# The range test of w1 and the squares of pairs 0 to 7 move from the first two stages to later fetches in the last ones

## The chip, the cores and the metric

The kernel runs on one core of a Trainium2 chip. The core has five engines, each with its own instruction stream: TensorE (PE in the profile; its weight loads are PEld), VectorE (DVE), ScalarE (ACT), GpSimd (POOL) and SyncE (SP). Data come from and go to device memory by DMA; here SP and POOL issue the transfers. The metric is the device time of one execution in microseconds (us), the median of several runs.

## The reference

A hashed attention over 4 batches, 8 heads, 768 rows and a head size of 64 gives x; a Fourier mixing block with two weight matrices works on x. Cut to what matters:

```python
mask = q_bucket[:, :, :, None] == k_bucket[:, :, None, :]     # 6 sign bits of q @ proj, k @ proj
scores = np.where(mask, scale * np.matmul(q, k.transpose(0, 1, 3, 2)), -1e9)
attn = softmax(scores)                                        # with the maximum subtracted
x = (attn @ v)  ->  (B, S, H*D)

u = x + np.real(np.fft.fft(np.fft.fft(x, axis=1), axis=2))
un = (u - mean) / np.sqrt(var + 1e-6)
out = u + np.maximum(un @ w_ch1, 0.0) @ w_ch2                 # w_ch1 512x2048, w_ch2 2048x512
```

Both weight matrices arrive as 64-bit floats. The kernel reads them as pairs of 32-bit words and makes 32-bit floats of them.

## The kernel before

The work is cut by batch. `attention(b)` handles the 4 head pairs of a batch (pair number n = 4b + t), each in 6 steps of 128 keys: `weigh` makes the scores (line 893; for the first pairs the mask is a product too, line 885), ACT takes their exp into one of two `pk` tiles (L897), and `values` multiplies by v (L914). The exp is taken without subtracting a maximum, which holds only for inputs of moderate size. `mix(b)` then does the Fourier part (`fold`, the products L1086 into F, L1115 into x) and `mlp7`, the two weight products in a scheme with seven products for eight. `mix(b)` of one batch is interleaved with `attention(b + 1)` by a counter in the main loop (L1500 to L1548). The last `mix(3)` has no attention beside it and runs alone: this is the last stage, from about 925 us on.

Two safety tests guard the fast path. If either fires, a slower general version of the whole computation (`_any_scores`) runs afterwards.

- The range test. `narrow` (L628) turns a raw slice of 128 x 512 double words into floats: two DVE instructions (L639, L643), one on ACT (L647), one on DVE (L649), and then, on ACT, the test: `Abs` of the high word (L654) and `Relu` of a threshold minus it (L655), summed into a column of `strange`. There are 16 slices of w1 (`weights1`, in the first stage, fetched by SP into seven raw buffers) and 16 of w2 (`weights2`, in the second stage, fetched by POOL, L693, into two).
- The norm test. `norm` (L748) squares a natural q or k tile of 128 x 768 on ACT (L750) and sums it into a column of `norms`; `prepare(n)` calls it for q and for k of each pair.

After the last attention, just before `mix(3)`, both tables are reduced (L1523 to L1538: two DVE reductions, three PE transposes, five small DVE instructions) to one flag, and `values_load` (L1539) puts it into a register of each engine.

Order. In the first stage (`attention(0)` with `weights1`, up to about 135 us) the order of PE, DVE, ACT and POOL is that of the program. From then on a scheduler in the compiler orders each engine's list at build time from its own estimates; the engines then run their lists in that order. SP's list is ordered by it throughout.

Buffers that matter. The tag `qkn` has two buffers for q and k tiles. The tag `z` has one: raw slices of w1, then z of each batch in turn (read by L1086), with raw slices of w2 in between. PSUM banks for products come from `pt` (L520): two banks normally; with `roomy` set (first stage's start, and from L1519 on) its requests rotate over three pools of two.

In `mlp7`, `inner(half)` has 4 row blocks in each half, of 7 products each (A11, S2, A12, S1, S3, S4, A22; L1390). ACT copies each result out of PSUM (L1412 c12, L1415 c21, L1419 c11, L1422 c22, L1427 and L1439 sd, L1431 c12), and A12, S4 and A22 add onto banks that must have been copied before. The left operands come from device memory by SP through a ring of 12 tiles (L1363). `outer7` has 8 products for each of 3 row pairs and half (L1270), with ACT copies L1289, L1300 and L1303 into `tq`. `across` transposes x into row tiles `un`, and ACT copies them out (L1142).

Of the kernel before, what the change touches and what calls it, by code (L numbers as in the profile page):

```python
# [20 lines left out]
P = 128  # L21
# [464 lines left out]
def _main(  # L486
# [27 lines left out]
    def wt(shape, dtype, tag, name, bufs=2):  # L514
        return work.tile(shape, dtype, tag=tag, name=name, bufs=bufs)
# [105 lines left out]


    least = const.tile([P, 1], F32, tag="least", name="least")
    nc.gpsimd.memset(least, float(897 << 20))
    strange = const.tile([P, 2 * NDC * DFF // WC], F32, tag="strange", name="strange")
    nc.gpsimd.memset(strange, 0.0)

    def narrow(dst, raw, col, low=None):  # L628


        lo, hi = (raw[..., i] for i in range(2))
        t = lo.bitcast(F32)
        if low is None:

            low, t = lo, hi.bitcast(F32)
        di = dst.bitcast(I32)


        nc.vector.tensor_scalar(  # L639
            di, hi, 3, (1 << 30) - 1,  # L640
            op0=ALU.logical_shift_left, op1=ALU.bitwise_and,
        )
        nc.vector.scalar_tensor_tensor(  # L643
            di, hi, -(1 << 30), di, op0=ALU.bitwise_and, op1=ALU.bitwise_or
        )

        nc.scalar.activation(low, lo.bitcast(U32), AF.Copy, scale=2.0**-29)  # L647
        if len(di.shape) == 2:
            nc.vector.tensor_tensor(di, di, low, op=ALU.add)  # L649
        else:  # L650
            for i in range(di.shape[1]):
                nc.vector.tensor_tensor(di[:, i], di[:, i], low[:, i], op=ALU.add)

        nc.scalar.activation(t, hi, AF.Abs)  # L654
        nc.scalar.activation(  # L655
            t, t, AF.Relu, bias=least, scale=-1.0, accum_out=strange[:, col : col + 1]
        )
# [22 lines left out]
    class Arrival:  # L680
# [19 lines left out]
        def convert(self, i, low=None):  # L700
            if self.wide:
                dst = self.slices[i][0]
                raw = self.raws[i % self.depth].bitcast(I32)
                if len(dst.shape) == 2:
                    raw = raw.rearrange("p (n w) -> p n w", w=2)
                else:
                    raw = raw.rearrange("p (s n w) -> p s n w", w=2, n=dst.shape[-1])
                narrow(dst, raw, self.col + i, low)
            self.fetch(i + self.depth)

    def weights1():
        slices = [
            (w1[:, c, f : f + WC], moe_w_ch1[c * P : (c + 1) * P, f : f + WC])
            for f in range(0, DFF, WC)
            for c in range(NDC)
        ]
        zt = wt([P, 3, 2 * WC], F32, "z", "zraw1", 1)
        ft = wt([P, 12, WC], F32, "F", "fraw", 1)
        raws = [zt[:, i] for i in range(3)] + [
            ft[:, i : i + 2].rearrange("p i w -> p (i w)") for i in range(0, 8, 2)  # L720
        ]
        arrival = Arrival(slices, raws, 0, nc.sync)
        for i in range(arrival.depth):
            arrival.fetch(i)
            if i == 1:
                load(1)
        yield
        half = None
        for i in range(len(slices)):
            arrival.convert(i, ft[:, 8 + i % 4].bitcast(I32))  # L730
            yield
            if half:
                centre(half[0], next(half[1]))
                half = None
            if i % NDC == NDC - 1:


                f = i // NDC * WC
                if f < DFF // 2:
                    half = f, average(f)  # L740
                    next(half[1])
# [2 lines left out]
    xs = {}  # L744

    preps = {}

    def norm(n, io, tn):  # L748
        junk = wt([P, S], BF16, "junk", f"sq{io}_{n}", 1)
        nc.scalar.activation(  # L750
            junk, tn, AF.Square,
            accum_out=norms[:, io, n : n + 1],
        )

    def prepare(n):
# [3 lines left out]
        for io, nm in enumerate("qk"):  # L759
            tn = nat.pop((nm, n))  # L760
            tt = wt([P, S], F32, nm + "t", f"{nm}t{n}")
            if n > 0:
                to, at = tt, tn
                if nm == "q":

                    to = tt.rearrange("p (i r n) -> p r i n", i=2, r=2)
                    at = tn.rearrange("p (r i n) -> p r i n", i=2, r=2)
                nc.vector.transpose(to, at)
            for g in range(2) if n == 0 else ():
                ps = pt([P, 3, P], f"tr{nm}{n}_{g}")  # L770
                for i in range(3):
                    c = 2 * i + g if nm == "q" else 3 * g + i
                    nc.tensor.transpose(ps[:, i, :], tn[:, c * P : (c + 1) * P], ident)
                if nm == "q":
                    for i in range(2):
                        dst = tt[:, i * HALF + g * HALF // 2 : i * HALF + (g + 1) * HALF // 2]
                        evac(
                            dst.rearrange("p (j c) -> p c j", c=3),
                            ps[:, :, i * D : (i + 1) * D],
                        )  # L780
                else:
                    evac(
                        tt[:, g * HALF : (g + 1) * HALF],
                        ps.rearrange("p c t -> p (c t)"),
                    )
            ts[nm] = tt
            yield
            norm(n, io, tn)
        if lite:


# [708 lines left out]
    for b in range(B):  # L1500
# [17 lines left out]
        if b == B - 1:  # L1518
            roomy[0] = True  # L1519

            ms = const.tile([P, 3], F32, tag="ms", name="ms")  # L1523
            nc.vector.tensor_reduce(ms[:, 0:2], norms, axis=AX.X, op=ALU.max)
            nc.vector.tensor_reduce(ms[:, 2:3], strange, axis=AX.X, op=ALU.max)
            ps = pt([1, 3, P], "norms_t")
            for io in range(3):
                nc.tensor.transpose(ps[:, io, :], ms[:, io : io + 1], ident)
            mt = const.tile([1, 5], F32, tag="mt", name="mt")
            nc.vector.tensor_reduce(mt[:, 0:3], ps, axis=AX.X, op=ALU.max)  # L1530
            nc.vector.tensor_tensor(mt[:, 3:4], mt[:, 0:1], mt[:, 1:2], op=ALU.mult)
            nc.vector.tensor_scalar(
                mt[:, 4:5], mt[:, 3:4], (SAFE / SCALE / 2) ** 2, None, op0=ALU.is_gt
            )
            fl = const.tile([1, 1], I32, tag="fl", name="fl")
            nc.vector.scalar_tensor_tensor(
                fl, mt[:, 2:3], 0.0, mt[:, 4:5], op0=ALU.is_gt, op1=ALU.max
            )  # L1538
            large = nc.values_load(fl[0:1, 0:1], min_val=0, max_val=1)  # L1539
        for _ in other:  # L1540
            pass
        other = mix(b)
        if b == 0:
            zt2 = wt([P, 3, 2 * WC], F32, "z", "zraw2", 1)
            arrival2 = weights2()
            other = after(2 + NT, other, islice(arrival2, HF + 1))
    for _ in other:
        pass  # L1548

    return large  # L1550

# [42 lines left out]
```

## Time and profile before

| | us |
|---|---|
| median of 3 runs (1101.38 to 1104.4) | 1102.72 |
| the profiled execution | 1102.7 |
| its span, first to last instruction | 1100.4 |
| PE busy | 1043.3 |
| DVE busy | 790.5 |
| ACT busy | 499.5 |
| POOL busy | 58.6 |

The groups that the change moves, from the answers on single lines (counts and median duration in ns): L654 Abs 32 x 686, L655 Relu 32 x 772, L750 square 32 x about 843. The counts of L654 and L655 include w2's 16 slices; w1's are those from 15.4 to 94 us. The squares of pairs 0 to 7 are 16 of the 32, from 7.3 to 182 us.

How to read it: a busy share is an average over stages with different limits, so each stage is looked at by itself. In a timeline a line gives start, duration, engine, line of the code and operation; the bracket at its end is the idle time of the engine before it and what ended that. In the table by windows the columns are the window, its length, then busy time of PE, PEld, DVE, ACT and POOL, the granted clock, the mean busy share of the 16 DMA engines and what they moved in GB/s.

### The profile page before, as it was taken

The page shows a single profiled execution, that of the slowest core. Times are in us where ns is not written, and L with a number is a line of the kernel's source. Part 1 is how long each engine was busy: PE and PEld are TensorE (multiplying, and loading weights), DVE is VectorE, ACT ScalarE, POOL GpSimd, SP SyncE. Part 2 cuts the span into 40 slices and gives each one's busy share as a digit, 9 for nine tenths or more (in the row PEclk, how much of TensorE's full clock was granted, in tenths as well). Part 3 has the DMA queues.
Part 4 walks back from the last instruction along what each step waited for, and adds up shares of the span by engine and source line. Part 5 has one row for each costly group of instructions (what it writes and reads, how often), then busy time and mean ns, then how long its engine had stood idle before and what let it go on. Part 6 is the DMA issues. An engine that isn't in the chain of part 4 may idle for free.

```text
span 1100.4 us, 14144 instructions
## 1 busy us (share of the span) xinstructions
PE 1043.3 (95%) x4933; PEld 632.7 (57%) x4933; DVE 790.5 (72%) x1336; ACT 499.5 (45%) x1055; POOL 58.6 (5%) x132
## 2 busy tenths in 40 slices
PE   7989897999989999999999999999999999999996
PEld 3333353446744675545664576645674569768575
DVE  5899958878599977776767785965856785644353
ACT  6987555553276324454326433355315522340420
POOL 0000000002000020010000011001000002100000
PEclk9999999999999999999999999999999999999998
DMA  9755353451056161322154134213032205122301
GB/s 222 224 95 126 64 140 72 138 164 19 20 149 209 44 204 26 68 63 66 26 157 107 48 82 153 44 43 92 15 129 68 68 24 172 55 81 88 123 20 41
DMA packets 175710, 103.13 MB, mean 94 GB/s; under 512 B 129552, under 2 KB 162960, under 8 KB 175632
## 3 DMA queue, kind: packets, MB, share of 16 engines
q1 hardware_dynamic: 169840, 88.65, 30.1%
q0 software_dynamic: 4224, 13.11, 3.7%
q8 instruction: 41, 0.67, 0.2%
q10 hardware_dynamic: 1568, 0.39, 0.2%
q14 instruction: 37, 0.30, 0.1%
HBM read 81.14 MB, written 20.97 MB: 93 GB/s over the span
## 4 chain that ended last, share of the span: by engine, by line
PE 61%; DVE 11%; ACT 4%; DMA 2%; issue 2%; DVEq 0%; SPq 0%; ACTq 0%
PE o L1270 22%; PE h_p L1390 20%; PE oo L914 6%; PE sc L893 6%; DVE pk L903 3%; PE cs L1086 2%; DMA zraw<-in_moe_w_ch_dram 2%; PE A L1115 2%; PE B L1115 1%; DVE acc L988 1%; ACT rr L948 1%; DVE w L1282 1%; DVE h L1256 1%; PE bits L825 1%; PE un L1141 1%
## 5 line engine op out<-in xcount | busy, mean ns | idle before, releaser
L1270 PE MATMUL o<-w,h 128*128 128x256 f32 x1152 | 259.4, 382 | 1.2 <-ACT tq L1289 0.7
L1270 PEld LDWEIGHTS o<-w,h 128*128 128x128 f32 x1152 | 216.3, 190 | 43.6 <-issue 4.6
L897 ACT ACTIVATE pk<-sc 128x768 f32<-128x768 f32 x192 | 147.6, 809 | 78.4 <-PE sc L893 60.9
L1390 PE MATMUL h_p<-x,w 128*128 128x384 f32 x448 | 163.5, 495 | 3.2 <-ACT h L1412 1.5
L893 PE MATMUL sc<-qt,kt 64*128 64x384 f32 x768 | 155.7, 508 | 6.0 <-ACT pk L897 5.7
L914 PE MATMUL oo<-pk,vn 128*64 128x385 f32 (+1 forms) x768 | 155.3, 499 | 6.0 <-DVE pk L903 3.0
L903 DVE SCALAR_TENSOR_TENSOR pk<-qb,kb,pk 128x768 f32<-128x768 bf16 x132 | 129.0, 1012 | 30.2 <-ACT pk L897 30.1
L1390 PEld LDWEIGHTS h_p<-x,w 128*128 128x128 f32 x448 | 82.3, 190 | 71.0 <-ACT pk L897 5.4
L988 DVE TENSOR_TENSOR acc<-acc,pk 128x1536 f32<-128x1536 f32 (+1 forms) x72 | 105.7, 1482 | 7.2 <-ACT pk L897 6.7
L1390 PE MATMUL h_p<-w 128*128 128x384 f32 x288 | 105.5, 489 | 2.3 <-ACT w L1427 2.3
L914 PEld LDWEIGHTS oo<-pk,vn 128*64 128x64 f32 x768 | 49.1, 136 | 100.0 <-issue 69.3
L893 PEld LDWEIGHTS sc<-qt,kt 64*128 64x128 f32 x768 | 66.9, 188 | 51.3 <-issue 24.0
L1390 PEld LDWEIGHTS h_p<-w 128*128 128x128 f32 x288 | 53.7, 190 | 41.7 <-ACT w L1427 3.5
L1300 ACT COPY tq<-o 128x256 f32<-128x256 f32 x24 | 8.9, 372 | 105.1 <-PE o L1270 105.1
L1282 DVE SCALAR_TENSOR_TENSOR w<-o,rs,w 128x256 f32<-128x256 f32 x56 | 26.7, 478 | 41.6 <-PE o L1270 41.6
L1270 PE MATMUL o<-w 128*128 128x256 f32 x176 | 42.3, 383 | 1.3 <-DVE w L1282 1.3
L1416 DVE TENSOR_TENSOR h<-h 128x384 f32<-128x384 f32 x32 | 17.8, 556 | 33.1 <-ACT h L1415 33.1
L1289 ACT COPY tq<-o 128x256 f32<-128x256 f32 x24 | 8.9, 371 | 69.3 <-PE o L1270 69.2
L1270 PEld LDWEIGHTS o<-w 128*128 128x128 f32 x176 | 32.8, 190 | 8.8 <-DVE w L1282 2.9
L1423 DVE TENSOR_TENSOR h<-h 128x384 f32<-128x384 f32 x32 | 17.7, 553 | 27.0 <-ACT h L1422 27.0
L1024 POOL DMA_DIRECT2D out_dram<-w x30 | 16.4, 548 | 388.7 <-issue 293.2
L1086 PE MATMUL cs<-ch,z 128*128 128x128 f32 (+3 forms) x192 | 33.2, 324 | 3.0 <-DVE bt L829 1.9
(170 smaller groups left out, 1312.4 us busy)
## 6 DMA issues: line engine op xcount, KB each, us to landing
w<-ad SPq DMA_DIRECT2D x168, 128.0 KB, 2.0
w<-bd SPq DMA_DIRECT2D x42, 512.0 KB, 4.5
zraw<-in_moe_w_ch_dram POOLq DMA_DIRECT2D x16, 512.0 KB, 4.0
bd<-w SPq DMA_DIRECT2D x14, 512.0 KB, 3.9
vn<-in_v_dram SPq DMA_DIRECT2D x32, 192.0 KB, 3.4
qn<-in_q_dram SPq DMA_DIRECT2D x120, 48.0 KB, 2.4
kn<-in_k_dram SPq DMA_DIRECT2D x60, 96.0 KB, 3.4
zraw<-in_moe_w_ch_dram SPq DMA_DIRECT2D x8, 512.0 KB, 5.7
```

What stands on the lines that cost most here:

```text
L893: last[0] = nc.tensor.matmul(ps[:, h, 0:HALF], kt[rows, ks], qt[rows, qs], start=kb is not None, stop=True,)
L897: nc.scalar.activation(pk[:, g, :, 0:HALF], ps[:, :, 0:HALF], AF.Exp, scale=SCALE)
L903: nc.vector.scalar_tensor_tensor(w, qb[:, h].rearrange("p (g s) -> p g s", g=2), kb[:, h, c : c + 1], w, op0=ALU.is_equal, op1=ALU.mult,)
L914: nc.tensor.matmul(oos[g][h * D : (h + 1) * D, 0:w], nat["v", n][:, (2 * c + h) * D : (2 * c + h + 1) * D], pk[:, g, h, 0:w], start=(c == ...
L988: nc.vector.tensor_tensor(acc[:, g], (first if c == 1 else acc)[:, g], new[:, g], op=ALU.add,)
L1086: nc.tensor.matmul(ps[:, pc + 2 * lo : pc + 2 * hi - 1 : 2], z[:, cp, pc, par, t * P : (t + 1) * P], ch[:, cp, pc, lo:hi], start=(cp == 0) ...
L1115: nc.tensor.matmul(ps[:, cols], F[:, par, k, t, j * P : (j + 1) * P], sq[:, t, k, cols], start=(t == 0), stop=(t == 1),)
L1270: nc.tensor.matmul(ps, a[:, r], right7[i][:, r], start=start and r == 0, stop=r == HF // 2 - 1, skip_group_check=not start,)
L1282: nc.vector.scalar_tensor_tensor(t[:, cols], src, r, t[:, cols], op0=ALU.mult, op1=ALU.add)
L1390: nc.tensor.matmul(ps, left[:, k], right[i][:, k], start=start and k == 0, stop=k == 1, skip_group_check=not start,)
L1416: nc.vector.tensor_tensor(c21, c12, c21, op=ALU.add)
L1423: nc.vector.tensor_tensor(c22, c21, c22, op=ALU.add)
```

## The change

The 16 range tests of w1's slices are no longer made when the slices are converted. `Arrival` is given no column (`None`), and `narrow` then leaves the test out. The test itself becomes a function `in_range`, which reads the high word as a 32-bit float instead of as an integer; the threshold is the same bit pattern read as a float. w2's tests stay where they were, in this form.

`prepare(n)` no longer squares q and k of pairs 0 to 7. Pairs 8 to 15 keep their squares.

A new generator `guard` makes up for both. It fetches q and k of pairs 0 to 7 a second time (16 transfers of 128 x 768 floats, 384 KB each, 3 KB in one piece per partition, issued by POOL into the `qkn` buffers) and squares each; it fetches the 16 raw slices of w1 a second time (512 KB each, by POOL, into three raw buffers in the `z` tag) and tests each; and it does the reductions and the flag. In the program it is stepped inside the loop over `mix(3)`; the register load of the flag follows at step 56 of 64.

```diff
-    nc.gpsimd.memset(least, float(897 << 20))
+    nc.gpsimd.memset(least, float(np.array(897 << 20, np.int32).view(np.float32)))
...
+        if col is not None:
+            in_range(raw, col, t)
...
+    def in_range(raw, col, t=None):
+        lo, hi = (raw[..., i].bitcast(F32) for i in range(2))
+        t = lo if t is None else t
         nc.scalar.activation(t, hi, AF.Abs)
         nc.scalar.activation(
             t, t, AF.Relu, bias=least, scale=-1.0, accum_out=strange[:, col : col + 1]
...
-        arrival = Arrival(slices, raws, 0, nc.sync)
+        arrival = Arrival(slices, raws, None, nc.sync)
...
+    LATER = 2 * NPAIR
+    def guard():
+        for n in range(LATER):
+            b, t = divmod(n, NPAIR)
+            for io, src in enumerate((q, k)):
+                tn = wt([P, S], F32, "qkn", f"nn{io}_{n}", 2)
+                nc.gpsimd.dma_start(
+                    tn,
+                    src[b, 2 * t : 2 * t + 2].rearrange("h (p c) d -> (h p) (c d)", p=P // 2),
+                )
+                norm(n, io, tn)
+                yield
+        if wide:
+            raws = wt([P, 3, 2 * WC], F32, "z", "zlast", 1)
+            for i, (dst, src) in enumerate(slices1()):
+                raw = raws[:, i % 3].bitcast(I32)
+                nc.gpsimd.dma_start(raw.bitcast(I64), src)
+                in_range(raw.rearrange("p (n w) -> p n w", w=2), i)
+                yield
...
+        yield fl
...
-            norm(n, io, tn)
+            if n >= LATER:
+                norm(n, io, tn)
...
-    for _ in other:
-        pass
+    checks = guard()
+    flag = None
+    for i, _ in enumerate(other):
+        if (i < 9 or i % 4 < 3) and flag is None:
+            flag = next(checks)
+        if i == MIX - 8:
+            large = nc.values_load(flag[0:1, 0:1], min_val=0, max_val=1)
```

What stands between the `if wide` part and `yield fl` are the reductions and the flag, unchanged, that stood before `mix(3)`.

More of the change, by code (lines that the diff above doesn't have):

```diff
@@ L652, in narrow @@
                 nc.vector.tensor_tensor(di[:, i], di[:, i], low[:, i], op=ALU.add)
+        if col is not None:
+            in_range(raw, col, t)
+    wide = moe_w_ch1.dtype == I64
+    def in_range(raw, col, t=None):
+        lo, hi = (raw[..., i].bitcast(F32) for i in range(2))
+        t = lo if t is None else t
         nc.scalar.activation(t, hi, AF.Abs)
@@ L707, in convert, with slices1 @@
                     raw = raw.rearrange("p (s n w) -> p s n w", w=2, n=dst.shape[-1])
-                narrow(dst, raw, self.col + i, low)
+                narrow(dst, raw, self.col and self.col + i, low)
             self.fetch(i + self.depth)
-    def weights1():
-        slices = [
+    def slices1():
+        return [
             (w1[:, c, f : f + WC], moe_w_ch1[c * P : (c + 1) * P, f : f + WC])
@@ L716, in weights1 @@
         ]
+    def weights1():
+        slices = slices1()
         zt = wt([P, 3, 2 * WC], F32, "z", "zraw1", 1)
@@ L746, in _main @@
     preps = {}
+    LATER = 2 * NPAIR
[17 more added lines that the diff above has]
+                yield
+        ms = const.tile([P, 3], F32, tag="ms", name="ms")
+        nc.vector.tensor_reduce(ms[:, 0:2], norms, axis=AX.X, op=ALU.max)
+        nc.vector.tensor_reduce(ms[:, 2:3], strange, axis=AX.X, op=ALU.max)
+        ps = pt([1, 3, P], "norms_t")
+        for io in range(3):
+            nc.tensor.transpose(ps[:, io, :], ms[:, io : io + 1], ident)
+        mt = const.tile([1, 5], F32, tag="mt", name="mt")
+        nc.vector.tensor_reduce(mt[:, 0:3], ps, axis=AX.X, op=ALU.max)
+        nc.vector.tensor_tensor(mt[:, 3:4], mt[:, 0:1], mt[:, 1:2], op=ALU.mult)
+        nc.vector.tensor_scalar(
+            mt[:, 4:5], mt[:, 3:4], (SAFE / SCALE / 2) ** 2, None, op0=ALU.is_gt
+        )
+        fl = const.tile([1, 1], I32, tag="fl", name="fl")
+        nc.vector.scalar_tensor_tensor(
+            fl, mt[:, 2:3], 0.0, mt[:, 4:5], op0=ALU.is_gt, op1=ALU.max
+        )
+        yield fl
     def norm(n, io, tn):
@@ L1519, in _main @@
             roomy[0] = True
[L1523 to L1539, printed above, removed]
         for _ in other:
```

## The prediction

> **What bounds the kernel now.** I read the page (busy shares, chain of waits) first, then the busy time by windows cut at stage borders, then the timelines of ScalarE (ACT) and VectorE (DVE) in the places that the change touches.
>
> ```profile
> PE 1043.3 (95%) x4933; PEld 632.7 (57%) x4933; DVE 790.5 (72%) x1336; ACT 499.5 (45%) x1055; POOL 58.6 (5%) x132
> ...
> PE 61%; DVE 11%; ACT 4%; DMA 2%; issue 2%; DVEq 0%; SPq 0%; ACTq 0%
> ```
>
> TensorE (PE) holds the chain. The exceptions, by windows (columns: length, then busy PE, PEld, DVE, ACT, POOL, clock, DMA share, GB/s):
>
> ```profile
> 41.00:68.40 27.40, 24.15 (x164) 9.35 (x162) 26.32 (x44) 23.47 (x48) 0.00 (x0) 1.00 0.63 130
> 68.40:99.00 30.60, 28.30 (x192) 11.11 (x190) 28.83 (x49) 29.94 (x64) 0.11 (x1) 1.00 0.50 98
> ...
> 135.00:190.00 55.00, 44.94 (x246) 26.89 (x246) 38.70 (x66) 30.33 (x64) 3.45 (x6) 0.96 0.41 106
> ...
> 932.00:945.00 13.00, 12.59 (x80) 12.14 (x80) 9.64 (x19) 1.65 (x6) 0.00 (x0) 1.00 0.00 1
> 945.00:957.00 12.00, 12.00 (x46) 7.48 (x45) 7.29 (x16) 7.22 (x16) 1.70 (x4) 1.00 0.27 78
> 957.00:970.00 13.00, 13.00 (x42) 7.64 (x41) 4.91 (x11) 6.42 (x14) 3.69 (x9) 1.00 0.33 102
> ```
>
> From 41 to 99 us ACT is nearly full, but so is DVE (its timeline shows back-to-back instructions, one gap of 0.28 us). From 945 PE is full, and ACT, half busy, empties each PSUM bank as its product ends. Prices and waits, from timelines:
>
> ```profile
> 50.54 0.69 ACT L654 ACTIVATE zraw<-zraw 128x512 f32<-128x512 int32 x1
> 51.27 0.81 ACT L655 ACTIVATE zraw<-zraw,least 128x512 f32<-128x512 f32 x1
> ...
> 52.04 1.50 ACT L897 ACTIVATE pk<-sc 128x768 f32<-128x768 f32 x2
> 53.42 0.85 ACT L750 ACTIVATE sq<-kn 128x768 bf16<-128x768 f32 x1
> ...
> 54.25 1.51 ACT L897 ACTIVATE pk<-sc 128x768 f32<-128x768 f32 x2
> ...
> 175.14 0.53 POOL L693 DMA_DIRECT2D zraw<-in_moe_w_ch_dram  x1 [10.93 <-ACT zraw L655]
> ...
> 179.06 0.70 ACT L647 ACTIVATE zraw<-zraw 128x512 int32<-128x512 uint32 x1 [4.22 <-DMA zraw<-in_moe_w_ch_dram]
> ...
> 944.40 0.59 ACT L1142 COPY w<-un 128x512 f32<-128x512 f32 x1 [11.35 <-PE un L1141]
> ...
> 948.50 0.49 ACT L1419 ACTIVATE h<-h_p 128x384 f32<-128x384 f32 x1 [0.81 <-PE h_p L1390]
> ```
>
> Start to next start: a test (Abs, Relu) holds ACT 1.50 us, a square 0.83. A POOL fetch of 512 KB takes 3.9 us, and ACT stands behind it.
>
> **The skill.** "Perfetto Trace Analysis", Tensor Engine Instruction, says ACT and DVE run strictly first in, first out; the wait at 179.06, with a score tile's exp ready behind it, agrees. "DMA: Bandwidth & Descriptors", Anatomy of one DMA, prices a POOL transfer at 2.0 us plus bytes/436e3: 3.2 us for 512 KB; the trace has a median of 4.0 and decides. "ScalarE: Activation LUTs", What ACT_TABLE_LOAD costs, charges per element, whatever the function; Abs 0.69 and Relu 0.77 on 512 elements fit, so reading the words as float should cost what reading them as integers does.
>
> **Part 1, taken away.** 16 tests x 1.50 and 16 squares x 0.83 = 37.3 us of ACT.
> - First stage, up to 135 us: all tests, 13 squares. DVE has gaps of 1.27, 1.66 and 2.43 us before 41 and 0.28 after; to 117 it is then full. The first waits on a conversion with no test ahead of it, the third on PE's sums, themselves behind DVE. Only the second (accumulation at 17.78, its exp queued behind a test until 16.96) closes, by about 1.1. Gain 1.2; bounds 0 and 3.
> - Second stage: two squares stand in the two-buffer ring of w2's fetches, at 172.48 and 181.14. Without them the fetch of 175.14 starts 0.8 earlier and the exp of 181.97 comes 1.65 earlier. The scheduler also puts a second exp ahead of the next waiting conversion (before: 186.13, with PE idle 2.66). Some returns where DVE builds the next operands. Gain 2.0; bounds -1 (reordering) and 8 (most of PE's 10 us idle in 135-190).
> - Before the last stage the reductions, three transposes and flag leave 900-903: about 1 us of DVE, which delayed ACT's rr copies. They return in the last stage's second inner half, where DVE has room. Gain 0.5; bounds 0 and 1.
>
> **Part 2, squares added.** In the changed program's lists they are not in the last mix: the scheduler puts them into the preceding one, ACT's list after the tq copy of 772.84, POOL's after the rs group that ends at 749.9. Two buffers: a fetch waits for the square two before. No row shows 384 KB through POOL. Taking 4.0 x 0.75 = 3.0 as low end and 4.0 as high, I use 3.4. A round of two squares then lasts 3.4 + 0.83 + 0.1 = 4.3 us. The first pair is there; seven rounds give 775 + 7 x 4.3 = 805, and with other work in the way about 809. Walking ACT's list against PE's (product 1.73 us, score or value group 1.45): the copy of o_0_0_6 comes 0.7 us after its bank is needed, that of o_0_1_4 1.3 after; the rest fit, since the scheduler spread attention steps out. Cost 2.0; bounds 0.5 and 6. POOL waits meanwhile; its next task, a store at 888, is far.
>
> **Part 3, tests added.** zlast takes z's buffer, free after the last cs matmul at 932.2. Three fetches go out at 0.53 us spacing. Two issued together at 151.13 were consumed at 155.85 and 157.44, so I let three land at 936.8, 938.4, 940.0. ACT is idle 933.05-944.40 and its list has six tests there: 936.8-941.5 for three; refetches from 938.4, 940.0, 941.6 take about 4.3 and land at 942.7, 944.3, 945.9, so the sixth ends at 947.4. The un copies start 3.0 late. Ten more tests are threaded between PSUM copies up to the third row block's c22 copy (970.3 before). ACT holds about 14.3 us of own work in 944.4-970.3 (7.2 + 6.4 + the ends); with 10 x 1.5 = 15 that is 29.3 in 25.9: 3.4 us over even without a gap. Walking the list with refetch waits (eighth 0.3, fourteenth 1.0) and waits on DVE sums, the copy ends near 977.8: 7.5 late, and PE's next accumulation needs it. Later ACT has 0.8 us free per product, but PE has none, so nothing is recovered. Cost 7.5; low end 1.4 + 3.4 - 0.3 = 4.5 (3.7 us fetches, perfect packing), high 14 (fetches at 5.6, as that of the second raw at 151.8). Cover elsewhere: POOL's rs results wait behind these fetches, but the outer products that need them start at 982; SP's flag load sits ahead of nine ring loads that are wanted a row block (7 products, 9 us) after the flag's; and 8.4 MB over 38 us make 220 GB/s beside the ring's 100, while the window 205-230 moved 234 at a DMA share of 0.65, so the engines just suffice.
>
> **Sum**, against this execution (span 1100.4, time 1102.7, the runs' median 1102.72): -1.2 - 2.0 - 0.5 + 2.0 + 7.5 = +5.8, so span 1106.2 and time **1108.5**.
>
> **Rivals.**
> - *Cancelled* (0.19): tests packed at 4.5, squares 0.5, gains 4.5: 1103.2. For it: six-bank PSUM rotation in the last stage lets PE run a product ahead. Against: c12's copy gates the product after next.
> - *Fetches slow under load* (0.12): 5.6 us each makes a square round 6.5, seven end at 820, 10 late; tests 11: -3.7 + 21 = 1120. For it: 7.5 us seen for the fetch of 163.68. Against: DMA carries about 1 GB/s at 790-810 and 932-945.
> - *Faster* (0.08): the second stage's w2 ring. If 8 of PE's 10 us idle return, with 2.0 of the first stage and 0.5, against costs at their low ends (5.0): -5.5, 1097.2. It decides once the gains pass 8.3. For it: ACT waited 23.3 us there on fetches. Against: the squares held only 1.65 of that ring, its own tests stay.
> - *The test fires* (0.01): the fallback runs and time doubles. The weights are random at a scale of 0.04; the threshold is 2^-126.
>
> **Numbers.** Forecast case 0.60. A measurement here tells 0.3%, 3.3 us, from none: the bounds are 1099.4 and 1106.0. Faster 0.08 (that rival); within 0.20 (most of cancelled, a little of the forecast's low side); slower 0.72. Range 1102.5 to 1117: the known bounds, leaving out the faster rival, the worst of the slow fetches, and the fallback.
>
> **What would show it.** First stage: DVE as full as before, about 1 us shorter. 770-812: sq instructions 2.2 us apart, PE gaps near 2 us. After the F copies: six tests, un copies 3 us late; the first inner half with ACT above 90% and PE idle of some 7 us. I am wrong if the first inner half keeps its length, or the first 230 us shorten by over 6.

## The result, and where the time went

Before 1102.77 us (median of 5 runs, 1101.38 to 1104.4), after 1115.96 us (median of 5, 1113.99 to 1119.01). The ratio is 1.0125, 95% interval 1.0106 to 1.0143: slower, inside the range given, but by 13.2 us where 5.8 were forecast. The profiled execution took 1115.4 us, its span is 1113.5.

The page of the kernel after, busy times and chain of waits:

```profile
PE 1050.3 (94%) x4933; PEld 632.6 (57%) x4933; DVE 789.8 (71%) x1336; ACT 499.8 (45%) x1055; POOL 76.2 (7%) x164
...
PE 20%; DMA 4%; DVE 2%; issue 2%; ACT 1%; POOL 1%; POOLq 0%; DVEq 0%; ACTq 0%
```

PE has the same 4933 products and 7 us more of busy time; ACT has as much work as before, only elsewhere. The chain is cut short (its shares add up to 30%), so its shares cannot be set against those of before; but the two transfers by which its DMA share goes, `nn` and `zlast`, are those that the change added. To see where they cost, I cut the span at five marks that exist in both programs and do not move against each other: the copy of the first outer product of the third `mix` (the copy at 772.84 before), the first copy of a weight product in its second half (827.33), the first F copy of the last stage (926.12), the first outer copy of the last stage (984.48), and the end. All numbers are start times in the timeline of ACT, subtracted.

| stretch, us | before | before, profiled again | after | squares only | w1 tests only | neither |
|---|---|---|---|---|---|---|
| start to outer copy (first two stages and more) | 772.84 | 770.52 | 771.02 | 769.95 | 772.84 | 770.69 |
| to weight product copy (squares are here) | 54.49 | 54.50 | 61.74 | 61.56 | 54.49 | 54.49 |
| to first F copy (flag was here) | 98.79 | 98.79 | 98.46 | 98.47 | 98.45 | 98.79 |
| to outer copy (tests are here) | 58.36 | 58.36 | 66.57 | 58.15 | 68.51 | 58.36 |
| to the end of the span | 115.92 | 115.73 | 115.71 | 115.77 | 115.71 | 115.77 |

Two things are to be seen. The last four rows repeat to 0.2 us between two executions of the kernel before, so for a stretch without the moved checks a difference is real. With them the stretches scatter more: four kernels with the same list of ACT in the squares' stretch (after, squares only, and two that follow) took 61.56, 61.74, 61.84 and 62.58 us there, and four with the same list in the tests' stretch (after, and three that follow) 66.57, 67.37, 67.63 and 68.69. The first row differs by 2.3 us between those same two executions, so a gain of that size in one profile means nothing. The loss has two places and no more: +7.25 us where the squares stand, +8.21 where the tests stand; 0.33 comes back from the flag and 0.21 in the last row.

The same stretches by windows of the kernel after (columns as before). The first three answer to the windows of the first two stages that were shown, the fourth holds the squares, the last two the tests:

```profile
41.00:68.40 27.40, 24.12 (x150) 8.68 (x148) 24.17 (x40) 13.91 (x26) 0.00 (x0) 0.88 0.65 131
68.40:99.00 30.60, 28.88 (x186) 11.15 (x186) 27.51 (x47) 19.23 (x40) 0.11 (x1) 0.94 0.39 82
135.00:190.00 55.00, 46.59 (x260) 27.22 (x256) 41.92 (x73) 30.20 (x63) 3.40 (x6) 1.00 0.43 113
769.20:831.00 61.80, 57.00 (x268) 38.16 (x267) 39.30 (x57) 27.35 (x62) 8.71 (x16) 0.97 0.48 154
...
937.20:953.60 16.40, 13.89 (x84) 12.57 (x82) 11.36 (x20) 9.75 (x22) 4.25 (x8) 1.00 0.69 226
953.60:983.00 29.40, 26.13 (x81) 14.97 (x82) 10.48 (x24) 25.83 (x61) 9.87 (x20) 0.94 0.72 236
```

From 41 to 99 us ACT lost 20 us of work and the stage did not become shorter: the granted clock is 0.88 and 0.94 where it was 1.00, and DVE, which was the next to be full, is idle 2.2 and 1.3 us more. From 769 to 831 PE is idle 4.8 us with ACT busy less than half of the time. From 953.6 to 983, ACT is busy 88% and PE idle 3.3 us. The granted clock is no cause of the two losses, though it fell in both places: in the kernel after it was 0.97 over the whole stretch of the squares, and two kernels with the same squares and 1.00 took as long (61.84 and 62.58 us); over that of the tests it was 0.97 too, and the kernel with the tests alone, at 1.00, took 68.51.

**The squares.** ACT, POOL and DVE in the timeline of the kernel after (start, duration, engine, line, operation; the bracket is the idle time before it and what ended it):

```profile
771.02 0.37 ACT L1342 COPY tq<-o 128x256 f32<-128x256 f32 x1 [2.02 <-PE o L1323]
773.88 0.84 ACT L802 ACTIVATE sq<-nn 128x768 bf16<-128x768 f32 x1 [2.49 <-DMA nn<-in_q_dram]
...
778.55 0.84 ACT L802 ACTIVATE sq<-nn 128x768 bf16<-128x768 f32 x1 [3.73 <-DMA nn<-in_k_dram]
...
779.39 0.35 ACT L1353 COPY tq<-o 128x256 f32<-128x256 f32 x1
...
784.04 0.84 ACT L802 ACTIVATE sq<-nn 128x768 bf16<-128x768 f32 x1 [2.00 <-DMA nn<-in_k_dram]
```

```profile
746.97 1.09 POOL L1205 TENSOR_TENSOR rs<-rs,mhalf 128x1 f32<-128x1 f32 x2
770.43 0.64 POOL L769 DMA_DIRECT2D nn<-in_q_dram  x1 [22.37 <-issue]
775.12 0.54 POOL L769 DMA_DIRECT2D nn<-in_k_dram  x1 [4.05 <-ACT sq L802]
776.12 0.54 POOL L769 DMA_DIRECT2D nn<-in_q_dram  x1 [0.46 <-DVE kt L820]
```

```profile
768.87 0.97 DVE L820 STREAM_TRANSPOSE qt<-qn 128x768 f32<-128x768 f32 x1
...
774.86 0.96 DVE L820 STREAM_TRANSPOSE kt<-kn 128x768 f32<-128x768 f32 x1
...
782.01 1.95 DVE L956 SCALAR_TENSOR_TENSOR pk<-qb,kb,pk 128x768 f32<-128x768 bf16 x2 [3.57 <-ACT vs L977]
```

```profile
784.51 5.41 PE L1323 MATMUL o<-w,h 128*128 128x256 f32 x16 [1.89 <-DVE rt L992]
```

POOL is done with its rs group at 748 and then stands 22 us: the two buffers hold q and k of the last pair, long squared (at 710.52 and 720.00) but transposed only at 768.87 and 774.86. So the first fetch leaves at 770.43, when q's buffer is free. The second, by its bracket, waits for the square made of the first and leaves at 775.12; only the third (776.12) waits for the transposition of k. The first two squares, which I had counted as ready, hold ACT 6.2 us. Behind them stand a copy (779.39, 8.4 us after the one at 771.02; 6.0 us before), two exps and a scale copy, for which DVE waits 3.57 us; PE then waits 1.89 us for DVE. After that the ring runs on; over all sixteen:

```profile
  ACT sq L802: 18.4, 14
...
DMA to landing us min/median/max: 3.1/3.3/4.8
```

ACT waited 18.4 us on these fetches in 14 waits. Each single fetch takes what I had assumed (3.4 us).

**The tests.** ACT in the timeline of the kernel after, from the end of the F copies:

```profile
942.21 0.68 ACT L663 ACTIVATE zlast<-zlast 128x512 f32<-128x512 f32 x1 [4.06 <-DMA zlast<-in_moe_w_ch_dram]
...
948.12 0.69 ACT L663 ACTIVATE zlast<-zlast 128x512 f32<-128x512 f32 x1 [1.42 <-DMA zlast<-in_moe_w_ch_dram]
...
950.70 0.67 ACT L663 ACTIVATE zlast<-zlast 128x512 f32<-128x512 f32 x1 [0.98 <-DMA zlast<-in_moe_w_ch_dram]
...
953.56 0.57 ACT L1195 COPY w<-un 128x512 f32<-128x512 f32 x1
...
982.51 0.47 ACT L1475 COPY h<-h_p 128x384 f32<-128x384 f32 x1
```

As forecast: six tests first, the un copies 4.06 us late (3.0 forecast), the third row block's c22 copy, the last line, 8.1 us late (7.5 forecast). "Late" is counted from the first F copy, 926.12 before and 931.22 after; the c22 copy of before starts at 969.30.

### The profile page after: what moved, and what is told of

The parts are those of the page before. It is cut to its first block, busy times and chain, and to the rows that moved or that the text cites. A ratio compares the mean times of both kernels' runs of the same rounds, so it can differ in the third digit from the quotient of the medians.

```text
span 1113.5 us, 14170 instructions
## 1 busy us (share of the span) xinstructions
PE 1050.3 (94%) x4933; PEld 632.6 (57%) x4933; DVE 789.8 (71%) x1336; ACT 499.8 (45%) x1055; POOL 76.2 (7%) x164
## 5 line engine op out<-in xcount | busy, mean ns | idle before, releaser
L1323 PE MATMUL o<-w,h 128*128 128x256 f32 x1152 | 262.1, 384 | 5.3 <-DVE rt L992 1.9
```

The lines of the kernel that those rows point to most:

```text
L1323: nc.tensor.matmul(ps, a[:, r], right7[i][:, r], start=start and r == 0, stop=r == HF // 2 - 1, skip_group_check=not start,)
```

## The experiments

**1. One half of the change at a time, and neither.** In the first kernel `Arrival` gets its column 0 back for w1 and `guard` makes no tests; in the second `LATER` is 0, so that all squares stay in `prepare`; in the third both loops of `guard` are empty. In this order:

```diff
-                narrow(dst, raw, self.col and self.col + i, low)
+                narrow(dst, raw, self.col + i, low)
...
-        arrival = Arrival(slices, raws, None, nc.sync)
+        arrival = Arrival(slices, raws, 0, nc.sync)
...
-        if wide:
+        if False:
```

```diff
-    LATER = 2 * NPAIR
+    LATER = 0
```

```diff
+    nc.gpsimd.memset(norms, 0.0)
...
-        for n in range(LATER):
+        for n in ():
...
-        if wide:
+        if False:
```

> Only the squares are moved; w1's range tests stay at the conversion. Theory A (each part costs where it stands: the squares by waiting on their fetches in the preceding mix, the w1 tests by filling ScalarE after z comes free): the squares cost the 7.25 us read from the marks of the two traces, the flag gives back 0.3 and the early stages at most 1: 1108.7 us (1107.5 to 1110). Rival B (the loss of the last stage follows from the first one, for instance because everything after it is out of step): most of the 13 us stay, 1113 or more.

> Only w1's range tests are moved; all squares stay in prepare. Theory A: the tests cost 8.1 us, the flag gives back 0.3, the first stage at most 1: 1109.8 us (1108.5 to 1111). Rival B: 1104 to 1106, since the tests alone would find ScalarE in step. If A holds, the differences of this run and of the run with the squares alone add up to that of the full change within about 1.5 us.

> The 16 squares and w1's 16 range tests are left out altogether (the flag is made from the other half); what remains is what taking them away is worth. Theory A (the first stage is bound by VectorE and by the granted clock of TensorE, so freed ScalarE time buys little): 1100.6 us, the 1.8 us seen at 771 us plus 0.3 of the flag. Rival C (my forecast's gain of 3.7 us is there but eaten by the added fetches before 771): 1099.0 us.

Measured, as ratios to before: squares only 1.0049 (1.0034 to 1.0063), tests only 1.0096 (1.0069 to 1.0124), neither 0.9997 (0.998 to 1.0014). In us of 1102.7 that is +5.4, +10.6 and -0.3. The two halves stand by themselves (rival B is out): the table above shows the squares' stretch 7.07 us longer without the tests, and the tests' stretch 10.15 longer without the squares. They add up to 16.0, not 13.8; I had allowed 1.5 us, and the intervals (1.6 us either way and 3.0) cover the rest. With the tests alone the compiler puts the un copies between the tests (22.1, 24.3 and 26.1 us after the first F copy) instead of behind the sixth (22.3, 22.8 and 23.3 in the kernel after), the second of them behind a wait of 1.00 us for a fetch. The third ratio is against my forecast: taking 32 operations off ACT is worth 0.3 us (a gain of 2.2 to a loss of 1.5), not 3.7; rival C is out, and theory A's gain of 2.1 lies at the edge of the interval.

**2. The squares without their fetches.** All sixteen squares are made of the first two tiles.

```diff
-                tn = wt([P, S], F32, "qkn", f"nn{io}_{n}", 2)
-                nc.gpsimd.dma_start(tn, ...)
-                norm(n, io, tn)
+                if n == 0:
+                    tn = wt([P, S], F32, "qkn", f"nn{io}_{n}", 2)
+                    nc.gpsimd.dma_start(tn, ...)
+                    tns.append(tn)
+                norm(n, io, tns[io])
```

> The full change, but only the first pair's q and k are fetched again, and the sixteen squares are all made of these two tiles (fourteen of the sixteen fetches, and the squares of seven pairs, are left out). Theory A (the squares cost by ScalarE waiting on the two-buffer ring): the wait for the first two fetches stays, 6.2 of 18.4 us of waiting; the other twelve go, and with them 4 of the 7.25 us: about 1112 us (1110.5 to 1113). Rival D (it is the squares' own ScalarE time and the changed order of the lists): 1116, as the full change.

Measured 1.0077 (1.0049 to 1.0105), some 5 us under the full change. The squares' stretch is 56.35 us, 1.86 over before, against 7.25 with the fetches. A window over this stretch, in this kernel and in the one before:

```profile
770.50:827.00 56.50, 54.43 (x271) 36.64 (x270) 38.74 (x60) 28.28 (x64) 0.60 (x2) 1.00 0.27 87
```

```profile
771.00:825.60 54.60, 54.05 (x268) 37.37 (x267) 38.94 (x59) 13.64 (x30) 0.00 (x0) 1.00 0.24 74
```

ACT does all the squares (28.3 us of work in 56.5, twice as much as before) and PE is idle 2.1 us instead of 0.6. So 5.4 of the 7.25 us hang on the fetches; ACT's own time and the new order of its list are the other 1.9. Rival D is out. (The compiler ordered ACT's list anew here: the copy of 776.53 stands ahead of the second square, for one, so that this kernel is rid of most of the first pair's wait too. The next experiment looks at the first pair by itself.)

**3. Is it the late start, or the pace?** q and k of the last pair go into a buffer that is idle then, so that the ring's two buffers come free at 701 instead of 769. In a second kernel the squares are also held behind the copy of the first outer product (an edge in ACT's order, no wait), so that they stay in their old place.

```diff
-            tl = wt([P, S], F32, tag, f"{nm}n{n}", bufs)
+            if n == NPAIR * B - 1 and nm != "v":
+                if nm == "q":
+                    held.append(wt([P, 2, S], F32, "ef", "qk15", 1))
+                tl = held[0][:, "qk".index(nm)]
+            else:
+                tl = wt([P, S], F32, tag, f"{nm}n{n}", bufs)
```

```diff
-            nc.scalar.copy(qq, p1)
+            first_tq.setdefault((b, half), nc.scalar.copy(qq, p1))
...
-                norm(n, io, tn)
+                with tc.issue_after(first_tq[2, 0].ins):
+                    norm(n, io, tn)
```

> The full change, but q and k of the last pair are loaded into another buffer that is idle then, so that the two buffers of the re-fetched tiles come free near 701 us instead of 769 and 775. The compiler then also puts the squares earlier, among the products and exps from about 700 us on. If the squares cost by their late start (the step of my prediction that the first pair is already there): most of the 5.4 us that the fetches cost return, ratio 1.008. If they cost by the pace of a two-buffer ring in which ScalarE waits in order for each fetch, wherever it stands: ratio 1.012 or more.

> As the run with the buffers free early, but the squares are held back behind the same copy as in the full change (the first outer product of the third mix, at 771 us), so that the first two tiles are fetched 60 us before their squares and only the place is kept. If the first pair's late start is what my forecast missed: the stretch from that copy to the weight products' copy, 61.74 us in the full change and 54.49 before, falls to about 56.5, and the ratio to 1.008. If it is the pace of the two-buffer ring from the second pair on: the two first waits go (6.2 us of 18.4), but the following waits grow, the stretch stays above 60, and the ratio is 1.011 or more.

The first measured 1.016 (1.0145 to 1.0176): nothing returned, but it doesn't answer the question. The compiler moved the squares forward with the buffers, to 705 to 748, among the products of the first half, and again put the first one ahead of its tile; it waited 4.08 us. From the scale copy of the pair before (706.66 before, 707.26 here) to the outer copy 73.36 us pass, 66.18 before: a cost of 7.2 in another place.

The second measured 1.0106 (1.0089 to 1.0123). Its stretch of the squares (768.43 to 827.83) is 59.40 us, a cost of 4.9, which lies between what the two theories gave, nearer to the second. (Its ratio fits the second too, but its tests' stretch, in which nothing was changed, took 68.69 us, 2.1 more than in the full change, so the stretch decides.) ACT in its timeline:

```profile
768.70 0.85 ACT L811 ACTIVATE sq<-nn 128x768 bf16<-128x768 f32 x1
...
769.67 0.85 ACT L811 ACTIVATE sq<-nn 128x768 bf16<-128x768 f32 x1
...
773.21 0.84 ACT L811 ACTIVATE sq<-nn 128x768 bf16<-128x768 f32 x1 [2.60 <-DMA nn<-in_q_dram]
...
790.09 0.84 ACT L811 ACTIVATE sq<-nn 128x768 bf16<-128x768 f32 x1 [1.44 <-DMA nn<-in_k_dram]
...
792.15 0.84 ACT L811 ACTIVATE sq<-nn 128x768 bf16<-128x768 f32 x1 [1.13 <-DMA nn<-in_q_dram]
...
793.00 0.35 ACT L1351 COPY tq<-o 128x256 f32<-128x256 f32 x1
```

The first pair is there now, and from the second on ACT waits as before, 12.3 us in 12 waits; the copy at 793.00 has two such waits ahead of it. With experiment 2 the 7.25 us fall into three: 2.3 for the late first pair (7.25 - 4.91), 3.0 for the pace of a ring of two buffers (4.91 - 1.86), in which a fetch can leave only when the square two back is done and ACT stands at each square until its tile has landed, and 1.9 for the squares themselves. These parts are good to about 1 us: the three kernels' lists also differ in where other squares and copies stand, and the same list scattered by 1.0.

**4. Tests: ACT's time or the fetches?** Two kernels. One fetches three slices and makes all sixteen tests on them; one fetches all and tests the first 256 words of each 512.

```diff
-                nc.gpsimd.dma_start(raw.bitcast(I64), src)
+                if i < 3:
+                    nc.gpsimd.dma_start(raw.bitcast(I64), src)
...
-                in_range(raw.rearrange("p (n w) -> p n w", w=2), i)
+                in_range(raw.rearrange("p (n w) -> p n w", w=2)[:, 0 : WC // 2], i)
```

> The full change, but only the first three slices of w1 are fetched again and the sixteen tests are made on these three (thirteen fetches, and the test of thirteen slices, are left out). Theory A (after the wait for the first three slices, ScalarE's own time sets the tests' cost: 24 us of tests and 14 of copies between 942 and 983): only the few microseconds of gaps return, about 2: ratio to before 1.0105 (1.009 to 1.012), about 2 us under the full change. Rival E (the waits on fetches set it, as with the squares): the 5.9 us of waiting after the first wait return: ratio 1.007.

> The full change with every slice of w1 fetched whole, but Abs and Relu taken over the first 256 of its 512 words (half of the words are left untested). ScalarE's time per test falls from 1.50 us to about 0.95, by 9 us in all; the number of waits and fetches stays. Theory A: the cost of the tests falls by about 5 us, from 8.2 to about 3: ratio 1.0078 (1.006 to 1.009). Rival E (the fetches set it): by 2 at most, ratio 1.011.

Measured: three fetches 1.0072 (1.0047 to 1.0096), half tests 1.0145 (1.0124 to 1.0167). The tests' stretch is 60.69 us without the refetches (+2.3) and 68.29 with half of the tests' work (+9.9). My theory A, that ACT's own time sets this cost, is wrong. Rival E has the first kernel; of the second it expected a gain of up to 2 us, and nothing was gained at all. 5.9 of the 8.2 us go with the refetches: ACT's waits for fetches fall from 10.0 us to 3.8, that for the first three slices. The line of the fetches, first in the kernel after, then in that with half tests:

```profile
L779 POOL DMA_DIRECT2D zlast<-in_moe_w_ch_dram x16: 530/530/621, 937.6 to 973.8; - x16
...
  ACT zlast L663: 10.0, 8
...
DMA to landing us min/median/max: 4.0/5.1/7.1
```

```profile
L779 POOL DMA_DIRECT2D zlast<-in_moe_w_ch_dram x16: 527/530/621, 940.8 to 976.9; - x16
...
  ACT zlast L663: 16.3, 10
...
DMA to landing us min/median/max: 4.1/4.9/6.4
```

The sixteen fetches are spread over 36.2 us in the one and 36.1 in the other. The two operations of a test became 0.47 us shorter (0.44 and 0.53 us, 0.68 and 0.76 before), 7.5 in all, and ACT's waiting grew from 10.0 to 16.3. So the waits took up what the tests gave back. That the stretch came out 1.7 us longer than in the full change says nothing: with whole tests and one and the same list it took 66.57 to 68.69 us in four kernels.

**5. The same checks where nobody waits for ACT.** The outer products of the last stage keep ACT busy 3.3 of 34 us. Two kernels move only the squares there (w1's tests stay at the conversion). A square is placed behind a copy of that stage (`issue_after`), and ACT itself issues the next fetch behind the square that frees the buffer; only the first two are POOL's. The first puts all sixteen into the first half's outer products, two or more behind most copies; the second puts one or two behind each copy there and the last four into the second half's (the last lines of the diff; `again` is one fetch).

```diff
+        tns = [again(0, 0), again(0, 1)]
+        yield
+        for n in range(LATER):
+            for io in range(2):
+                with tc.issue_after(last_tq[0].ins):
+                    norm(n, io, tns.pop(0))
+                    if n + 1 < LATER:
+                        tns.append(again(n + 1, io))
+                yield
...
-            nc.scalar.copy(qq, p1)
+            last_tq[0] = nc.scalar.copy(qq, p1)
...
+        n = 1 if i == 0 else 0
+        if 26 <= i < 38 and (i - 26) % 4 < 3:
+            n = 2 if (i - 26) % 4 == 0 else 1
+        if 52 <= i < 60 and (i - 52) % 4 < 3:
+            n = 1
```

> A version that may beat both: the range tests stay at the conversion; the squares of pairs 0 to 7 are moved, but into the outer products of the last stage's first half (985 to 1018 us), where ScalarE has 3 us of work in 33; ScalarE itself issues each fetch after the square that frees its buffer, so that nothing else waits behind a fetch on GpSimd. Theory A (squares cost only where ScalarE is waited for): the gain of the second stage, 2 to 3 us, stays, and the flag's 0.3: ratio 0.9975 (0.996 to 0.999). If the waits on fetches delay the nine copies there, PE idles and the ratio is 1.000 to 1.003.

> As the run with the squares in the outer products, but with one square behind most of the copies there and the last four in the second half's outer products, so that no square is waited for by a product: every fetch has two intervals between copies, about 7 us, to land, and none is left when the next weight products begin. Theory F (a moved square costs nothing where ScalarE reaches it after its fetch has landed): ScalarE's waits on fetches nearly vanish, the last stage is as long as before within 0.5 us, and what is left is the gain of taking the squares out of the first two stages, 1 to 3 us in the profile: ratio 0.998 (0.9965 to 1.0005). Rival G (the added transfers slow the operands of the last stage): 1.003 or more.

Measured: all in the first half 1.0067 (1.0053 to 1.008), spread 0.9989 (0.9979 to 1.0000). The first is worse than both theories gave: the copies were in time, but the ring was 6 us too slow for the stage (ACT waited 18.9 us on it), and two squares were left when the next weight products began. Its timeline of ACT:

```profile
1020.61 0.84 ACT L811 ACTIVATE sq<-nn 128x768 bf16<-128x768 f32 x1 [2.58 <-DMA nn<-in_q_dram]
...
1021.45 0.46 ACT L1474 COPY h<-h_p 128x384 f32<-128x384 f32 x1
...
1023.41 0.84 ACT L811 ACTIVATE sq<-nn 128x768 bf16<-128x768 f32 x1 [1.12 <-DMA nn<-in_k_dram]
```

PE waited 2.83 us for the copy at 1021.45, and the last row of the table became 119.9 instead of 115.9. (This execution, 1104.4 us, was the shortest of five, whose median is 1109.0; what the others lost beside it no profile shows.) With the squares spread, the timeline of ACT in the second kernel reads

```profile
986.38 0.37 ACT L1362 COPY tq<-o 128x256 f32<-128x256 f32 x1 [2.10 <-PE o L1332]
986.65 0.85 ACT L811 ACTIVATE sq<-nn 128x768 bf16<-128x768 f32 x1
...
987.62 0.34 ACTq L769 DMA_DIRECT2D nn<-in_q_dram  x1
988.11 0.37 ACT L1365 COPY tq<-o 128x256 f32<-128x256 f32 x1 [0.52 <-PE o L1332]
988.38 0.85 ACT L811 ACTIVATE sq<-nn 128x768 bf16<-128x768 f32 x1
```

All tiles but one (a wait of 1.44 us at 1012.37) have landed when ACT comes to them, and the last two rows are 57.83 and 116.05 us (58.36 and 115.92 before). The refetch of 6.3 MB and sixteen squares cost nothing. The row of the tests is 0.53 shorter than before, which I put down to the flag, whose reductions now come later still; it was not tried. A lead of 0.1% whose interval touches 1 is no more than a tie with the kernel before.

**6. The whole change in the outer products.** Three tests and three squares to each row pair, fetched by ACT; `guard` otherwise as in the second kernel of 5, w1's tests out of the conversion.

```diff
+        for what in "TS S TTS".split() * 5 + ["TS"]:
+            with tc.issue_after(last_tq[0].ins):
+                for w in what:
+                    if w == "T":
+                        in_range(raw.rearrange("p (n w) -> p n w", w=2), i)
+                        if i + 3 < 16:
+                            more(i + 3, nc.scalar)
+                    else:
+                        norm(n, io, tns.pop(0))
```

> The whole change, all 16 squares and all 16 tests of w1 on tiles fetched again, but in the outer products of the last stage, three tests and three squares to each row pair, each fetch issued by ScalarE behind the check that frees its buffer. Theory F (a check costs nothing where ScalarE reaches it after its fetch has landed and no copy waits behind it): the last stage keeps its length within 1 us; ratio 0.999 (0.997 to 1.001), against 1.0125 for the same checks in the change as made. Rival G (8.4 and 5.5 MB more in about 95 us slow the operands, or the fetches land late and hold ScalarE's copies): 1.004 or more, with PE waiting in the outer products.

Measured 0.9998 (0.9983 to 1.0013): the same thirty-two checks on the same refetched data, some 14 us cheaper than in the change as made. In the code each string is what stands behind one copy (T a test, S a square), and `more` fetches a slice. In its profiled execution (1106.8 us, the second longest of 14) ACT still stood once for a transfer, told in the last section, and the last row was 120.2 us.

**7. Why taking work away gained nothing.** The clock of 0.88 in the windows above made me think that PE, better fed before 41 us, is then throttled. This kernel is the one with neither, squares and tests left out, but the tests of the first five slices stay.

```diff
-                narrow(dst, raw, self.col and self.col + i, low)
+                narrow(dst, raw, self.col + i if self.col or i < 5 else None, low)
```

> The 16 squares and eleven of w1's sixteen tests are left out altogether; the tests of the first five slices, those up to 41 us, stay at the conversion. Theory H (taking the tests out makes TensorE so dense before 41 us that its clock is then lowered, to 0.87 or 0.94 from 41 to 98 us, which eats the gain): with the early tests kept the clock from 41 to 98 us stays 1.00, the first stage ends 3 to 5 us earlier than before, and the ratio is 0.995 (0.993 to 0.9975), lower than with all tests left out (0.9997). Rival I (VectorE bounds the first stage, the clock only fills its waits): ratio 0.998 to 1.0, and the mark at the end of the first stage is within 2 us of before.

> The kernel before, profiled once more. Theory K (the lowered clock between 41 and 98 us belongs to kernels without w1's tests): 1.00 in both windows again and the mark at the end of the first stage at 113 us. Rival L (it falls by chance, execution by execution, in any of them): 0.94 or lower in one of them, and the mark later than 113.

Measured 1.0006 (0.9992 to 1.0019), with the clock at 0.94 from 41 to 68 us: theory H falls, and so does the idea that a few tests kept would save the clock. Before, profiled once more, has 1.00 in both windows. The profiles side by side (the start of the fourth pair's scale copy is about the end of the first stage):

| kernel | clock 41-68 | clock 68-98 | stretches at half clock | fourth scale copy | outer copy |
|---|---|---|---|---|---|
| before; again | 1.00; 1.00 | 1.00; 1.00 | 0; 0 | 113.08; 113.71 | 772.84; 770.52 |
| squares out: only; in outer; spread | 1.00; 1.00; 0.94 | 1.00; 1.00; 1.00 | 0; 0; 1 | 110.17; 110.67; 110.94 | 769.95; 771.83; 770.98 |
| squares and late tests out (this kernel) | 0.94 | 1.00 | 1 | 111.31 | 771.65 |
| both out: three fetches | 1.00 | 1.00 | 0 | 108.07 | 765.85 |
| both out: one fetch; all in outer; early fetch, same place | 0.94; 0.94; 0.94 | 1.00; 1.00; 1.00 | 1; 1; 1 | 109.48; 109.94; 109.66 | 770.53; 774.00; 768.43 |
| both out: neither; half tests | 0.94; 0.94 | 0.94; 0.94 | 2; 3 | 111.41; 114.38 | 770.69; 774.10 |
| both out: after; buffers free early | 0.87; 0.87 | 0.94; 0.94 | 3; 3 | 112.06; 112.60 | 771.02; 780.62 (squares before it) |
| tests out only | 0.87 | 0.94 | 3 | 115.57 | 772.84 |

The means of 0.87 and 0.94 hide what happens: in all fifteen traces the clock is either full or half, and from the first 20 us to the end of the products a stretch at half lasts 3.41 us or twice that (counted as two in the table, which counts up to the fourth scale copy). Here are 3 us of the kernel after, then of the one with three fetches, with the line of PE ahead of each, the same eight matmuls behind the same wait:

```profile
55.79 1.94 PE L673 MATMUL ws<-w,ones 128*32 128x512 f32 x8 [3.28 <-DVE qkb L858]
...
56.00:59.00 3.00, 3.00 (x14) 0.79 (x8) 2.92 (x6) 1.15 (x2) 0.00 (x0) 0.50 0.28 45
```

```profile
55.77 1.06 PE L673 MATMUL ws<-w,ones 128*32 128x512 f32 x8 [3.28 <-DVE qkb L859]
...
56.00:59.00 3.00, 3.00 (x24) 1.15 (x18) 2.92 (x7) 2.09 (x4) 0.00 (x0) 1.00 0.30 46
```

PE is busy throughout in both, but has 14 matmuls in one and 24 in the other. A stretch of 3.41 us at half clock can cost 1.7 us, and the nine programs without w1's tests (last five rows), whose first stage is the same but for the squares in the last, line up by it: 108.07 us with none, 109.5 to 109.9 with one, 111.4 with two, 112.1 and more with three. So taking both out is worth 5.0 us of the first stage when the clock stays full, and in the kernel after, with three stretches at half, only 1.0 of them is left.

Each drop to half, in all fifteen traces, follows a gap of PE: in the 3.41 us before it PE had stood idle for at least 1.6 us. Here the gap is the wait of 3.28 us for DVE in the lines above. All ten programs without w1's later tests have it near 53 us; with all tests in, PE's waits are spread, and the longest between 41 and 68 us was 1.6 or 1.7 us in four traces and 2.4 in the fifth, the one with 0.94. So PE's clock was lowered behind a gap, and not because PE was dense before it. The gap alone doesn't decide it, as the kernel with three fetches shows: the changes of the clock lie on a grid of 3.41 us in each trace, and there the gap falls across a point of the grid, with 1.8 us of idle time on one side and 1.5 on the other; in the other nine one side has 1.96 us or more. That fits all ten, but nothing was run to move the grid. What is gained by 113 us is in part lost again by 771, where the two executions of before differ by as much as most of these kernels do.

## Why the prediction was right in sign and too small

- **First two stages, -3.2 forecast.** Too large. -1.8 in the profile, within the scatter of two executions of before; by the medians of the kernel with neither, 0.3 (the flag's stretch is 98.79 there, as before, so this is without the flag). At full clock the first stage gains more than the 1.2 I gave it (2.9 with the squares out, 5.0 with both), so ACT was more in its way than I read from DVE's busy time. But I had put the clock at nothing: with three stretches at half clock 4.0 of the 5.0 were gone again, and the second stage gave nothing that is clear of its scatter. There I added up waits of ACT (1.65 us at one exp, a wait of 2.66 for PE) as if they would shorten it by 2.0: from the fourth scale copy to the sixth (113.08 to 245.68) it is 132.6 us before, 129.7 before profiled again, 131.6 after.
- **Flag, -0.5 forecast.** 0.33 before the last stage and 0.21 in its end: right.
- **Squares, +2.0 forecast, 0.5 to 6 allowed.** 7.25: this is the step that failed, the price of the waits. Fetch (3.3 us), round (4.6 against 4.3) and even the end (812.6 against 809) were about right; two sentences were not. "The first pair is there" was false, since a buffer is free after its last reader, the transpose, not after the square: 2.3 us. "The rest fit" was false too: I walked ACT's list against PE's with the squares' own time and a few tenths of lateness, and a list without refetches costs indeed 1.9, but the waits of the later rounds add 3.0. They stand in ACT's one queue, and what is behind them is needed by DVE (rt, pk) and PE (tq). The Trainium skill's "Perfetto Trace Analysis", Tensor Engine Instruction, calls ACT and DVE strictly first in, first out, and this trace agrees (the copy of 779.39 stands behind waits of 2.49 and 3.73 us); I cited it and then priced the waits as if most copies could go round them.
- **Tests, +7.5 forecast, 4.5 to 14 allowed.** 8.2, right in size and place, and partly for a wrong reason. I took it for ACT's 24 us of tests beside 14 of copies; halving the tests shortened nothing, dropping the refetches left 2.3. So its size is in part luck, as a sum of work that doesn't set it came out near. (The copy that I put at 970.3 starts at 969.30, too.) The fetch landed in 5.1 us in the median (three in flight), where I had 4.3; the price that "DMA: Bandwidth & Descriptors", Anatomy of one DMA, gives for 512 KB on POOL is 3.2, and the trace decides.
- **Sum.** +7.35 of error: 5.25 from the squares, 1.4 from the first stages, 0.7 from the tests. The rival "fetches slow under load" had the nearer outcome (1120) with a mechanism that wasn't there for the squares: their fetches landed in 3.3 us, about as I took them.

## What to carry to other kernels

A fetch and its consumer in an engine's list cost that engine the time by which the list reaches the consumer before the data: count each round of the ring (issue, landing, consumer) against the distance of the consumers in the list, and take all that stands behind the wait as late by the difference. Here less work per item didn't help and an earlier start only once; more distance between consumers did, and the same 32 checks cost 15 us or nothing by where they stood. Before you count a gain from one profile, profile the kernel twice: a stretch that differs by 2 us between two executions can't show a gain of 2. And where a window's clock is below 1, look in it for single stretches at half clock, and for the gap of PE ahead of them.

## What the runs showed of the hardware

ACT stood for a transfer of SP's queue before it could issue its own. In the kernel of experiment 6, in ACT's timeline, and then all fetches of that line (shortest, median and longest issue in ns):

```profile
1021.64 5.57 ACTq L779 DMA_DIRECT2D zlast<-in_moe_w_ch_dram  x2
1027.26 0.84 ACT L824 ACTIVATE sq<-nn 128x768 bf16<-128x768 f32 x1 [6.10 <-DMA w<-bd]
...
1028.10 0.46 ACT L1487 COPY h<-h_p 128x384 f32<-128x384 f32 x1
```

```profile
L779 ACTq DMA_DIRECT2D zlast<-in_moe_w_ch_dram x13: 334/334/335, 987.3 to 1077.5; - x13
```

The 5.57 us are two issues of 0.33 us, the second at 1026.88, and a wait between them: ACT's list has a wait for a semaphore ahead of the second issue, it ends at 1026.82, and the semaphore (number 107) got its last count at 1026.80 from a load of the next right operands (w<-bd) that SP had issued at 1018.96. The fetch counts its own landing on the same semaphore. So it was not the issue that took long: in this program two transfers of different queues share a semaphore, and the later one is held until the earlier has landed. The copy behind it was late, PE was idle 1.94 us, and 3.41 us at half clock followed.

The granted clock was full or half; the half came in stretches of 3.41 us behind idle time of PE (1.6 us or more in the 3.41 us before, in fifteen traces), and such stretches go with most of the 6 us between the ends of the first stage of kernels whose first stage is the same program. They also make PE look busier: the kernel after has 20.5 us at half clock before its end and the kernel before 6.8, and half of the difference is the 7 us of busy time that PE has more.
